# Longformer attention and a gated feed-forward block on one core: scores by two 64-row matmuls in row tiles, and another order of the opening

## The chip, the cores and the metric

The kernel runs on one core of a Trainium2 chip. The metric is the device time of one execution in microseconds (us). The engines are TensorE (matmuls; its weight loads are a row of their own), VectorE, ScalarE, GpSimd and SyncE (which issues DMAs); each takes its instructions in program order. Matmuls write to PSUM, eight banks of 128 partitions x 512 fp32 values; ScalarE and VectorE read them from there.

## The reference

Attention with a window of 32 to each side and 8 global positions, for 8 batches x 8 heads of 576 positions x 64, then a feed-forward block over all 4608 tokens.

```python
def _attn_ref(q, k, v, global_idx):
    scores = scale * np.matmul(q, k.transpose(0, 1, 3, 2))
    mask = np.abs(pos[:, None] - pos[None, :]) <= 32
    mask = mask | is_global[:, None] | is_global[None, :]
    scores = np.where(mask, scores, -1000000000.0)
    attn = softmax(scores)
    return np.matmul(attn, v)

def _moe_ref(x, w_in, w_out):        # x: 4608 x 512
    h = x @ w_in                     # 512 x 2048
    g = h * np.cos(h)
    return g @ w_out                 # 2048 x 512
```

## The kernel before

**Tiles.** Heads are worked on in pairs: 32 pairs, four to a batch, the two heads of a pair in partitions 0 to 63 and 64 to 127. The queries of a pair are cut into 11 blocks of 56, with the 8 global queries ahead of each block (C = 64 columns); the keys of a block are 128 rows: 8 global ones and a window of 120. In `kw` the two heads' keys lie under each other. In `qb` each head has its own half, and the other head's partitions are zero there, so that one matmul over 128 rows gives both heads' scores of a block.

**Scores, values, turn.** `scores(pr, g)` (line 517) takes four blocks at a time: four matmuls into one bank of tag "s", an exponential on ScalarE, a product with the mask on VectorE into `pm`. `values(pr)` (531) multiplies `pm` with the values `vw` in 22 matmuls, each with 64 columns of weights, so that even and odd blocks use different column halves of the array; VectorE then sums, inverts and scales into `xn`. `turn_x(pr)` (552) transposes `xn` into `xT`; at the last pair of a batch GpSimd copies eight columns of global rows.

**Feed-forward.** `xT` is cut into 9 tiles of 512 tokens. `mlp_in(t, f)` is four matmuls of 512 columns into a bank of tag "h" (two of them), `mlp_act` a cosine on ScalarE and a product on VectorE into `g`, which has two buffers. `mlp_out(t, u)` is a quarter of a sum over 16 blocks for 128 tokens, four matmuls of 512 columns into `po`; the first quarter takes the bank of tag "o" (one bank; "s" too in the tail and where `spare` is set), the fourth copies `po` out, on ScalarE for odd and on VectorE for even blocks of tokens. Below, four such matmuls are a **unit**.

**PSUM.** Three banks "s", two "h", one "o", two for `pv`.

**Order.** It is written out by hand, as strings of steps that are issued as they stand. The opening `FRONT` makes pairs 0 to 7: `k`, `q` bring a pair's keys and queries to their places (transposes on TensorE, copies on ScalarE and VectorE), `C` casts values, `w` (`spread`, 361) lays out values by matmuls with 0/1 matrices, `s`, `p`, `x` are scores, values and turn; `L`, `W`, `O`, `K`, `B`, `A`, `c` issue loads (GpSimd's queue, for `A` and `B` SyncE's), `g` copies global rows on GpSimd, `m` and `t` are `mlp_in` and `mlp_act`. Then come passes 3 to 15. Pass 3 (`MID`) has no attention but keys and queries for the next pairs; passes 4 to 15 work on two pairs each, `a` and `z`, with `FOURTH`, `FIFTH`, `SIXTH` and else `ORDER`. There a "1" is a unit of `mlp_in` with its activation, and a "2" a unit of `mlp_out`; `n` squares `xn` on ScalarE for a later check, `G` issues casting DMAs. The steps "1" and "2" do nothing where their conditions fail:

```python
if ins_q and ins_q[0][0] < ready[0] and ins_q[0][0] < outs_q[0][0] + 2:        # "1"
...
if outs_q and need <= ready[1] and (tail[0] or NTT * NF - len(outs_q) < outs_by[0]):   # "2"
```

so a "1" is at most two token tiles ahead of the first "2" that is open. What is left of the 144 + 144 units runs in the tail, "1" and "2" in turn.

Of the kernel before, what the change touches and what calls it, by code (L numbers as in the profile page):

```python
# [9 lines left out]
FP32 = mybir.dt.float32  # L10
FP16 = mybir.dt.float16
I32 = mybir.dt.int32
AF = mybir.ActivationFunctionType
# [6 lines left out]
P = 128  # L20
# [178 lines left out]
def kernel(  # L199
# [138 lines left out]

    def hold(pr):

        nc.gpsimd.tensor_copy(gate, qb[pr % NK][0:1, 0, 0, G : G + 1])

    def vn16(s):
        return xT[:, s, 6 * TT : 9 * TT].rearrange("p (i n) -> p i n", i=NVT)
# [16 lines left out]
    def spread(pr):  # L361

        new, h0 = vn16(pr // 2), 2 * (pr % 2) * D
        for g0 in range(0, NB, 4):
            n = min(4, NB - g0)
            t = ps.tile([P, 4, P], FP32, tag="s", bufs=3)
            for j in range(g0, g0 + n):
                i = j // 2
                parts = ((2, i), (3, i + 1)) if j % 2 else ((0, i), (1, i - 1))
                nc.tensor.matmul(t[:, j - g0], own[:, pr], vg16[:, 0].rearrange("p h d -> p (h d)"), start=True, stop=False)  # L370
                parts = [(a, x) for a, x in parts if x >= 0]
                for a, x in parts:
                    m = min(VT, S - VT * x)
                    nc.tensor.matmul(t[:, j - g0], shift[0:m, a], new[0:m, x, h0 : h0 + 2 * D],  # L374
                                     start=False, stop=(a, x) == parts[-1])
            copy = nc.vector.tensor_copy if g0 == 4 else nc.scalar.copy
            copy(vw[pr % NV][:, g0 : g0 + n, :, 0:D], t[:, 0:n].rearrange("p n (h d) -> p n h d", h=2))

# [4 lines left out]
                view(vg16[(pr % 16) * G : (pr % 16 + 1) * G, pr // 16, h], (0, NB), (1, D)))  # L383


    mask = keep.tile([P, NB, 2, C], FP16)

    def build_mask():

        kid = work.tile([P, NB], FP32, tag="kid", bufs=1)  # L390
        nc.vector.tensor_copy(kid, kid_i)
        gf = work.tile([P, G], FP32, tag="gf", bufs=1)
        nc.vector.tensor_copy(gf, view(gidx_all, (2, G)))
        eq = work.tile([P, NB, G], FP32, tag="eq", bufs=1)
        nc.vector.tensor_tensor(eq, view(kid, (1, NB), (0, G)), view(gf, (0, NB), (1, G)), ALU.is_equal)
        isg = work.tile([P, NB], FP32, tag="isg", bufs=1)
        nc.vector.tensor_reduce(isg, eq, AX.X, ALU.max)
        ge0 = work.tile([P, NB], FP32, tag="ge0", bufs=1)
# [16 lines left out]
        for h in range(2):  # L415
            nc.vector.tensor_tensor(
                mask[:, :, h, G:], view(nk, (1, NB), (0, QB)), view(band[:, G:], (0, NB), (1, QB)), ALU.mult)
            nc.vector.tensor_scalar(
                mask[:, :, h, 0:G], view(val, (1, NB), (0, G)), own[:, 0:1], None, ALU.mult)
# [11 lines left out]
        for h in range(2):  # L431
            nc.vector.tensor_copy(mask[0:G, :, h, G:], view(one, (0, NB), (0, QB)))


    qgT = keep.tile([P, B * NP, G], FP16)
# [44 lines left out]

    def globals_q(pr):
        qp = qb[pr % NK]
        nc.gpsimd.tensor_copy(qp[0:D, 0, :, 0:G], view(qgT[0:D, pr], (0, NB), (1, G)))
        nc.gpsimd.tensor_copy(qp[D:P, 1, :, 0:G], view(qgT[D:P, pr], (0, NB), (1, G)))

    def turned(src, pr, n):

# [14 lines left out]
            nc.vector.tensor_copy(to, view(kT[pr // 2 % 2][:, pr % 2], (QB, NB), (1, W)))  # L502

    def local_q(pr):
        if pr < 2 * HY:
            t = turned(qn[pr // 2 % 2], pr, QP)
        for h in range(2):
            hp = slice(h * D, (h + 1) * D)
            to = qb[pr % NK][hp, h, :, G:]
            if pr < 2 * HY:  # L510
                copy = nc.scalar.copy if h == 0 or pr == 1 else nc.vector.tensor_copy
                copy(view(to, (C, NB), (RW, QB // RW), (1, RW)),  # L512
                     view(t[hp], (QB // RW, NB), (1, QB // RW), (QP, RW)))
            else:
                nc.vector.tensor_copy(to, view(qT[pr // 2 % 2][hp, pr % 2], (QB, NB), (1, QB)))  # L515

    def scores(pr, g):
        kp, qp = kw[pr % NK], qb[pr % NK]
        if g == 0:
            pm_of[pr] = work.tile([P, NB, 2, C], FP16, tag="pm", name="pm")  # L520
        pm = pm_of[pr]
        g0, n = 4 * g, min(4, NB - 4 * g)
        st = ps.tile([P, 4, P], FP32, tag="s", bufs=3)
        for j in range(n):
            nc.tensor.matmul(st[:, j], kp[:, g0 + j], view(qp[:, :, g0 + j], (NB * C, 2), (1, C)), start=True, stop=True)  # L525
        e = work.tile([P, 4, P], FP16, tag="e", bufs=3)
        nc.scalar.activation(e[:, :n], st[:, :n], AF.Exp, scale=scale)  # L527
        nc.vector.tensor_tensor(  # L528
            view(pm[:, g0], (1, n * P)), view(e, (1, n * P)), view(mask[:, g0], (1, n * P)), ALU.mult)

    def values(pr):
        pm, vp = pm_of.pop(pr), vw[pr % NV]
        for j in range(NB):
            for h in range(2):
                r0 = (j % 2) * C
                c0 = ((j // 2) % 3) * 130 + h * 65
                nc.tensor.matmul(pv[r0 : r0 + C, j // 6, c0 : c0 + 65], pm[:, j, h], vp[:, j, h],  # L537
                                 start=True, stop=True)
        den = pv[:, :, D : D + 1]
        rp = r_all[:, pr]  # L540
        dg = work.tile([G, 2], FP32, tag="dg")
# [10 lines left out]
    def turn_x(pr):  # L552
# [2 lines left out]
        if p == 0:  # L555
            xg_of[b] = work.tile([P, NP, G], FP16, tag="xg", name="xg")
        xg = xg_of[b]
        tx = ps.tile([P, BP, P], FP16, tag="o" if front[0] else "s", bufs=1 if front[0] else 3)
        for n in range(BP):
            nc.tensor.transpose(tx[:, n], xn[:, n], ident16)  # L560
        with nc.allow_low_precision("six rows of fp16"):
# [133 lines left out]
    with tc.manual_schedule():  # L695
# [14 lines left out]
        gather(k, kg32, 0)  # L710
        gather(q, qg32, 0)
        gather(v, vg32, 0)
        for t in (kn[1], qn[1], qb[2], qb[3]):
            nc.scalar.memzero(t.rearrange("p a b c -> p (a b c)"))
        load_qk(1)
        for i in range(2):
            nc.vector.memset(qb[i], 0.0)
        build_shifts()
        for i in range(NV):
            nc.vector.memset(vw[i][:, :, :, D : D + 1], 1.0)  # L720
# [53 lines left out]
                 "w": spread, "C": cast_vn, "V": lambda _: hold(9), "A": later_rows, "D": later_globals, "O": load_w_out, "K": lambda s: cast_half(s, "kq" if s == 4 else "vkq"), "B": bring, "m": lambda _: one(False), "t": lambda _: mlp_act()}  # L774
        ready[0] = 1
        for step in FRONT.split():
            f = (STEPS | OTHER)[step[0]]
            f(*[int(x) for x in (step[1:] or "0").split(".")])
        ready[0], front[0] = 2, False
# [85 lines left out]
```

## Time and profile before

| | us |
|---|---|
| median of 3 runs | 370.12 (365.66 to 370.38) |
| profiled run | 371.58 |
| its span | 369.8 |
| TensorE busy | 335.9 (91%) |
| VectorE busy | 266.3 (72%) |
| ScalarE busy | 249.5 (67%) |
| GpSimd busy | 105.9 (29%) |
| pass 3 begins (first steps behind the opening) | 72.4 |
| pass 4 begins | 87.95 |
| tail begins | 290.3 |
| last matmul ends | 363.4 |

The page gives busy time by engine, the span in 40 slices of 9.2 us, a chain of work followed back from the last instruction, and groups of instructions by line. Views of the trace give busy time in chosen stretches, instructions in order of time for one engine, and the same chain in order of time. A line such as `171.88 0.61 PE st L525 x11` reads: from 171.88 us on, for 0.61 us, eleven matmuls of line 525 that write `st`. In groups, `out<-in partitions x elements xcount | busy us, mean ns of one | idle before`.

### The profile page before, as it was taken

The numbers are of one execution on the slowest core, as the hardware profiler recorded it, in microseconds if no ns is written. First come the engines' busy times: TensorE is split into PE (matmuls) and PEld (weight loads), VectorE is DVE, ScalarE is ACT, GpSimd is POOL, SyncE is SP. The second block draws the span as 40 slices with busy tenths as digits, with TensorE's granted clock in tenths as the row PEclk, the third lists the DMA queues.
The fourth block names the chain that finished last, engine by engine and source line by source line (L and its number), as shares of the span: only waits on it lengthen the run. The fifth ranks groups of instructions, "written<-read, shape, count | busy, mean of one in ns | idle before, by whom it ended". The sixth has DMA issues, their size and how long they took to land.

```text
span 369.8 us, 8014 instructions
## 1 busy us (share of the span) xinstructions
PE 335.9 (91%) x2934; PEld 184.9 (50%) x2934; DVE 266.3 (72%) x615; ACT 249.5 (67%) x384; POOL 105.9 (29%) x239
## 2 busy tenths in 40 slices
PE   0399883999998999999999999999999999999992
PEld 0277673545553545555555555555555444444441
DVE  7659974696888888888888888888878445455410
ACT  5488882679776677778777868677787756644300
POOL 6735670161335250705253252603000100000000
PEclk9999997899999999999999999999999999999999
DMA  5979999999999999999999999999920000100111
GB/s 92 197 129 159 180 165 107 198 176 147 102 161 105 194 126 195 125 169 138 195 161 159 160 142 165 160 202 118 130 59 31 28 30 28 57 30 28 53 64 65
DMA packets 176280, 45.57 MB, mean 123 GB/s; under 512 B 164937, under 2 KB 171337, under 8 KB 176041
## 3 DMA queue, kind: packets, MB, share of 16 engines
q1 hardware_dynamic: 112601, 27.61, 58.3%
q0 software_dynamic: 63632, 17.37, 50.3%
q8 instruction: 25, 0.41, 0.5%
q14 instruction: 22, 0.18, 0.2%
HBM read 45.07 MB, written 20.05 MB: 176 GB/s over the span
## 4 chain that ended last, share of the span: by engine, by line
PE 79%; DVE 6%; issue 5%; ACT 3%; POOL 3%; DMA 2%; POOLq 0%; ACTq 0%
PE po L595 32%; PE ph L578 30%; PE st L525 5%; PE pv L537 4%; PE tx L560 2%; PE t L374 2%; DMA qn<-in_q_dram 2%; DVE g L585 2%; ACT e L527 1%; PE t L370 1%; PE t L492 1%; PE pn L628 1%; DVE xn L548 1%; POOL q L262 1%; ACT qb L512 1%
## 5 line engine op out<-in xcount | busy, mean ns | idle before, releaser
L584 ACT ACTIVATE cos<-ph,pio 128x512 f16<-128x512 f32 x144 | 97.1, 687 | 66.3 <-PE ph L578 64.7
L595 PE MATMUL po<-w_out,g 128*128 128x512 f16 x576 | 141.6, 379 | 0.0
L578 PE MATMUL ph<-xT,w_in 128*128 128x512 f16 x576 | 140.1, 379 | 0.3 <-DVE g L585 0.2
L585 DVE TENSOR_TENSOR g<-cos,ph 128x512 f16<-128x512 f16 x144 | 95.9, 685 | 46.9 <-ACT cos L584 44.9
L595 PEld LDWEIGHTS <-g 128*128 128x128 f16 x576 | 55.2, 98 | 62.1
L578 PEld LDWEIGHTS <-w_in 128*128 128x128 f16 x576 | 53.6, 98 | 60.5 <-issue 1.3
L527 ACT ACTIVATE e<-st 128x512 f16<-128x512 f32 (+1 forms) x96 | 47.9, 561 | 15.5 <-PE st L525 9.4
L528 DVE TENSOR_TENSOR pm<-e,mask 128x512 f16<-128x512 f16 (+1 forms) x96 | 37.2, 405 | 22.8 <-ACT e L527 21.0
L752 POOL COPY gate<-xn 1x1 f16<-1x1 f16 x12 | 2.2, 181 | 132.3 <-DVE xn L548 132.3
L525 PE MATMUL st<-qb,kw 128*128 128x128 f16 x352 | 29.2, 223 | 9.4 <-issue 5.0
L525 PEld LDWEIGHTS <-kw 128*128 128x128 f16 x352 | 24.1, 100 | 19.8 <-issue 9.1
L548 DVE TENSOR_TENSOR xn<-pv,r_all 128x768 f16<-128x768 f32 x32 | 30.7, 958 | 1.7
L568 POOL COPY xT<-xg 128x4 f16 x64 | 19.6, 306 | 28.7 <-DVE xT L563 25.3
L262 POOL DMA_DIRECT2D q<-in_q_dram x12 | 26.2, 2181 | 0.0
L614 ACT ACTIVATE sq<-xn 128x1536 f16<-128x1536 f16 x16 | 23.6, 1476 | 0.0
L515 DVE COPY qb<-qT 64x616 f16<-64x616 f16 x48 | 22.1, 460 | 0.3
L374 PE MATMUL t<-xT 112*128 112x128 f16 (+1 forms) x168 | 21.1, 240 | 0.7 <-ACT xT L349 0.4
L600 ACT COPY o<-po 128x512 f32<-128x512 f32 x18 | 10.5, 586 | 15.5 <-PE po L595 15.1
L262 POOL DMA_DIRECT2D k<-in_k_dram x12 | 19.8, 1646 | 0.0
L370 PE MATMUL t<-vg,xT 128*128 128x128 f16 x88 | 18.4, 242 | 0.9 <-issue 0.6
L537 PE MATMUL pv<-vw,pm 128*64 128x65 f16 x704 | 18.5, 199 | 0.0
L602 DVE COPY o<-po 128x512 f32<-128x512 f32 x18 | 12.3, 685 | 6.9 <-PE po L595 6.9
(123 smaller groups left out, 326.8 us busy)
## 6 DMA issues: line engine op xcount, KB each, us to landing
out_dram<-o SPq DMA_DIRECT2D x36, 256.0 KB
vw<-v SPq DMA_DIRECT2D x35, 165.0 KB
v<-in_v_dram POOLq DMA_DIRECT2D x12, 288.0 KB, 4.3
k<-in_k_dram POOLq DMA_DIRECT2D x12, 288.0 KB, 9.2
q<-in_q_dram POOLq DMA_DIRECT2D x12, 288.0 KB, 15.8
vn<-in_v_dram SPq DMA_DIRECT2D x20, 112.0 KB
w_in<-in_moe_w_in_dram POOLq DMA_DIRECT2D x4, 512.0 KB, 12.3
w_out<-in_moe_w_out_dram POOLq DMA_DIRECT2D x1, 2048.0 KB
```

The costliest lines, as they stand in the source:

```text
L262: nc.gpsimd.dma_start(dst[s].rearrange("t (h d) -> t h d", h=4), dview(src, base, (D, S), (S * D, 4), (1, D)))
L374: nc.tensor.matmul(t[:, j - g0], shift[0:m, a], new[0:m, x, h0 : h0 + 2 * D], start=False, stop=(a, x) == parts[-1])
L525: nc.tensor.matmul(st[:, j], kp[:, g0 + j], view(qp[:, :, g0 + j], (NB * C, 2), (1, C)), start=True, stop=True)
L527: nc.scalar.activation(e[:, :n], st[:, :n], AF.Exp, scale=scale)
L528: nc.vector.tensor_tensor(view(pm[:, g0], (1, n * P)), view(e, (1, n * P)), view(mask[:, g0], (1, n * P)), ALU.mult)
L537: nc.tensor.matmul(pv[r0 : r0 + C, j // 6, c0 : c0 + 65], pm[:, j, h], vp[:, j, h], start=True, stop=True)
L548: nc.vector.tensor_tensor(view(xn, (384, 2), (D, 6), (1, D)), view(pv, (512, 2), (65, 6), (1, D)), view(rp, (6, 2), (1, 6), (0, D)), ALU.mult)
L578: nc.tensor.matmul(ph, w_in16[:, j, f * P : (f + 1) * P], xT[:, j, t * TT : (t + 1) * TT], start=(j == 0), stop=(j == NC - 1))
L584: nc.scalar.activation(cos, ph, AF.Sin, bias=pio2)
L585: nc.vector.tensor_tensor(g, cos, ph, ALU.mult)
L595: nc.tensor.matmul(po, g16[:, f, s * P : (s + 1) * P], w_out16[:, f], start=(f == 0), stop=(f == NF - 1))
L614: nc.scalar.activation(sq, view(xn, (1, 2 * BP * P)), AF.Square, accum_out=x_sq[:, s : s + 1])
```

## The change

The zeros in `qb` go: both heads' queries lie under each other as the keys do, and a block's scores are two matmuls over 64 partitions each, one in the upper and one in the lower rows of the array. Each head has banks of its own: two for the blocks 0 to 7 and two for 8 to 10, three of them of tag "s" and one of tag "h" ("o" in the opening). A pair's scores are one step now. The exponentials are two of 512 and two of 192 columns. The values take even and odd blocks in turn, `spread` joins its matmuls, `mask` has one head, and all order strings are new.

```diff
-ORDER = "sa0 sa1 sa2 2 2 2 sz0 2 sz1 sz2 pa 1 1 2 xa pz G 1 1 2 xz n 1 1 2 kc qc 1 kd qd 2 1"
+ORDER = "sa 2 2 2 sz pa 1 1 2 xa pz G 1 1 2 xz n 1 1 2 kc qc 1 kd qd 2 1"
-FOURTH = "2 2 sa0 sa1 sa2 2 sz0 2 sz1 sz2 pa 1 1 2 xa pz G 1 1 2 xz n 1 1 2 kc qc 1 kd qd 2 1"
-FIFTH = "sa0 sa1 sa2 2 2 2 sz0 2 sz1 sz2 pa 1 2 xa pz G 1 2 xz n 1 2 kc qc 1 kd qd 2"
-SIXTH = "sa0 sa1 sa2 2 2 2 sz0 2 sz1 sz2 pa 1 1 2 xa pz G 1 1 2 xz n 1 1 D0 2 kc qc D1 1 kd qd D2 2 1"
-FRONT = ("s0.0 s0.1 s0.2 k1 q1 C0 w0 s1.0 s1.1 s1.2 L2 p0 k2 q2 C1 w1 x0 s2.0 s2.1 s2.2 W0 p1 k3 q3 C2 w2 x1 "
-         "s3.0 s3.1 s3.2 L3 W1 A g4 g5 p2 k4 q4 w3 x2 s4.0 s4.1 s4.2 g6 g7 c4 K4 W2 W3 p3 k5 q5 C3 w4 x3 s5.0 s5.1 s5.2 p4 k6 q6 w5 x4 n0 "
-         "s6.0 s6.1 s6.2 K5 p5 k7 q7 w6 x5 B4 s7.0 s7.1 s7.2 O p6 w7 n1 x6 m p7 m x7 t t")
+FOURTH = "2 2 sa 2 sz pa 1 1 2 xa pz G 1 1 2 xz n 1 1 2 kc qc 1 kd qd 2 1"
+FIFTH = "sa 2 2 2 sz pa 1 2 xa pz G 1 2 xz n 1 2 kc qc 1 kd qd 2"
+SIXTH = "sa 2 2 2 sz pa 1 1 2 xa pz G 1 1 2 xz n 1 1 D0 2 kc qc D1 1 kd qd D2 2 1"
+FRONT = ("s0 k1 q1 C0 w0 s1 L2 k2 q2 C1 w1 p0 s2 W0 k3 q3 x0 C2 w2 p1 s3 L3 W1 A g4 g5 k4 q4 x1 w3 p2 "
+         "s4 g6 g7 c4 K4 W2 W3 k5 q5 x2 C3 w4 p3 s5 k6 q6 x3 w5 p4 s6 K5 k7 q7 x4 w6 p5 s7 B4 O w7 x5 n0 p6 + m m x6 p7 t t m m x7 t t n1 -")
...
-    qb = [keep.tile([P, 2, NB, C], FP16, name=f"qb{i}") for i in range(NK)]
+    qb = [keep.tile([P, NB, C], FP16, name=f"qb{i}") for i in range(NK)]
...
-            for j in range(g0, g0 + n):
-                i = j // 2
-                parts = ((2, i), (3, i + 1)) if j % 2 else ((0, i), (1, i - 1))
-                nc.tensor.matmul(t[:, j - g0], own[:, pr], vg16[:, 0].rearrange("p h d -> p (h d)"), start=True, stop=False)
...
+            nc.tensor.matmul(view(t, (1, n * P)), own[:, pr], view(vg16[:, 0].rearrange("p h d -> p (h d)"), (0, n), (1, P)),
+                             start=True, stop=False, skip_group_check=True)
+            for a, j, k, x in runs:
+                m = min(VT, S - VT * x)
+                nc.tensor.matmul(view(t[:, j], (2 * P, k), (1, P)), shift[0:m, a], new[0:m, x : x + k, h0 : h0 + 2 * D],
+                                 start=False, stop=(a, j, k, x) == runs[-1], skip_group_check=True)
...
-        nc.gpsimd.tensor_copy(qp[0:D, 0, :, 0:G], view(qgT[0:D, pr], (0, NB), (1, G)))
-        nc.gpsimd.tensor_copy(qp[D:P, 1, :, 0:G], view(qgT[D:P, pr], (0, NB), (1, G)))
+        nc.gpsimd.tensor_copy(qp[:, :, 0:G], view(qgT[:, pr], (0, NB), (1, G)))
...
     def local_q(pr):
+        to = qb[pr % NK][:, :, G:]
         if pr < 2 * HY:
             t = turned(qn[pr // 2 % 2], pr, QP)
+            copy = nc.scalar.copy if pr % 2 else nc.vector.tensor_copy
+            copy(view(to, (C, NB), (RW, QB // RW), (1, RW)),
+                 view(t, (QB // RW, NB), (1, QB // RW), (QP, RW)))
+        else:
+            nc.vector.tensor_copy(to, view(qT[pr // 2 % 2][:, pr % 2], (QB, NB), (1, QB)))
+
+    def scores(pr):
+        kp, qp = kw[pr % NK], qb[pr % NK]
+        pm = pm_of[pr] = work.tile([P, 2, NB, C], FP16, tag="pm", name="pm")
+        tags = (("s", 3), ("s", 3), ("s", 3), ("o", 1) if front[0] else ("h", 2))
+        st = [ps.tile([P, 512], FP32, tag=tag, bufs=bufs, name="st") for tag, bufs in tags]
+        for j in range(NB):
+            for h in range(2):
+                hp = slice(h * D, (h + 1) * D)
+                nc.tensor.matmul(st[j // 8 * 2 + h][:, j % 8 * C : j % 8 * C + C], kp[hp, j], qp[hp, j], start=True, stop=True)
         for h in range(2):
-            hp = slice(h * D, (h + 1) * D)
...
+            e = work.tile([P, 512], FP16, tag="e", bufs=3)
+            nc.scalar.activation(e, st[h], AF.Exp, scale=scale)
+            nc.vector.tensor_tensor(view(pm[:, h], (1, 512)), e, view(mask, (1, 512)), ALU.mult)
+        e = work.tile([P, 512], FP16, tag="e", bufs=3)
+        n = (NB - 8) * C
+        for h in range(2):
+            nc.scalar.activation(e[:, h * n : (h + 1) * n], st[2 + h][:, 0:n], AF.Exp, scale=scale)
+        nc.vector.tensor_tensor(view(pm[:, 0, 8], (NB * C, 2), (1, n)), view(e, (n, 2), (1, n)), view(mask[:, 8], (0, 2), (1, n)), ALU.mult)
...
-        for j in range(NB):
+        for j0 in range(0, NB, 2):
             for h in range(2):
...
-        tx = ps.tile([P, BP, P], FP16, tag="o" if front[0] else "s", bufs=1 if front[0] else 3)
+        tx = ps.tile([P, BP, P], FP16, tag="s", bufs=3)
...
-        for t in (kn[1], qn[1], qb[2], qb[3]):
+        for t in (kn[1], qn[1]):
...
-        for i in range(2):
-            nc.vector.memset(qb[i], 0.0)
```

`spare`, set between "+" and "-", lets two of four `mlp_in` steps take a bank of tag "s". `MID` and the limits `outs_by` (8 more "2" with each pass) are as before.

More of the change, by code (lines that the diff above doesn't have):

```diff
@@ L339, in hold @@
     def hold(pr):
-        nc.gpsimd.tensor_copy(gate, qb[pr % NK][0:1, 0, 0, G : G + 1])
+        nc.gpsimd.tensor_copy(gate, qb[pr % NK][0:1, 0, G : G + 1])
     def vn16(s):
@@ L383, in load_vg @@
                 view(vg16[(pr % 16) * G : (pr % 16 + 1) * G, pr // 16, h], (0, NB), (1, D)))
-    mask = keep.tile([P, NB, 2, C], FP16)
+    mask = keep.tile([P, NB, C], FP16)
     def build_mask():
@@ L414, in build_mask @@
         nc.vector.memset(own[0:G], 0.0)
[L415 to L419, printed above, removed]
+        nc.vector.tensor_tensor(
+            mask[:, :, G:], view(nk, (1, NB), (0, QB)), view(band[:, G:], (0, NB), (1, QB)), ALU.mult)
+        nc.vector.tensor_scalar(
+            mask[:, :, 0:G], view(val, (1, NB), (0, G)), own[:, 0:1], None, ALU.mult)
         gc = work.tile([G, 1], FP32, tag="gc", bufs=1)
@@ L430, in build_mask @@
         nc.vector.tensor_scalar(one, one, 0.5, None, ALU.is_le)
-        for h in range(2):
-            nc.vector.tensor_copy(mask[0:G, :, h, G:], view(one, (0, NB), (0, QB)))
+        nc.vector.tensor_copy(mask[0:G, :, G:], view(one, (0, NB), (0, QB)))
     qgT = keep.tile([P, B * NP, G], FP16)
@@ L504, in local_q @@
     def local_q(pr):
+        to = qb[pr % NK][:, :, G:]
         if pr < 2 * HY:
             t = turned(qn[pr // 2 % 2], pr, QP)
-        for h in range(2):
-            hp = slice(h * D, (h + 1) * D)
[L509 to L529, printed above, removed]
+            copy = nc.scalar.copy if pr % 2 else nc.vector.tensor_copy
@@ L531, in values @@
     def values(pr):
         pm, vp = pm_of.pop(pr), vw[pr % NV]
-        for j in range(NB):
+        for j0 in range(0, NB, 2):
             for h in range(2):
[L535 to L538, printed above, removed]
+                for j in range(j0, min(j0 + 2, NB)):
+                    r0 = (j % 2) * C
+                    c0 = ((j // 2) % 3) * 130 + h * 65
+                    nc.tensor.matmul(pv[r0 : r0 + C, j // 6, c0 : c0 + 65], pm[:, h, j], vp[:, j, h],
+                                     start=True, stop=True)
@@ L776 @@
         for step in FRONT.split():
+            if step in "+-":
+                spare[0] = step == "+"
+                continue
+            if step in "+-":
+                spare[0] = step == "+"
+                continue
             f = (STEPS | OTHER)[step[0]]
```

10 lines of the change are left out of this document (5 added, 5 removed).

## The prediction

> **What bounds the kernel now.** I read the engine slices and the chain of waits first, then busy time by stage, then one middle pass on TensorE, ScalarE and VectorE. The page:
>
> ```profile
> PE   0399883999998999999999999999999999999992
> ...
> PE 79%; DVE 6%; issue 5%; ACT 3%; POOL 3%; DMA 2%; POOLq 0%; ACTq 0%
> ```
>
> TensorE carries the chain; its only hole after the first slices is the 3 in slice seven. By stage (opening until 72.40, then pass 3, passes 4 to 15, the tail):
>
> ```profile
> 16.70:57.25 40.55, 35.60 (x696) 29.91 (x696) 31.26 (x76) 33.54 (x56) 23.02 (x44) 1.00 1.23 158
> 57.25:62.29 5.04, 0.00 (x0) 0.00 (x0) 0.75 (x3) 0.00 (x0) 0.00 (x0) 0.85 1.72 86
> 62.29:72.40 10.11, 9.44 (x108) 6.89 (x108) 5.86 (x17) 6.42 (x10) 0.00 (x0) 0.74 1.68 185
> 72.40:87.95 15.55, 15.32 (x71) 6.74 (x69) 13.87 (x26) 12.57 (x20) 8.62 (x24) 1.00 1.66 167
> 87.95:290.30 202.35, 200.48 (x1691) 107.12 (x1690) 170.71 (x388) 153.55 (x229) 63.24 (x149) 1.00 1.38 140
> 105.48:121.21 15.73, 13.97 (x127) 7.27 (x126) 13.35 (x30) 11.95 (x18) 5.59 (x12) 1.00 1.41 146
> 155.58:172.50 16.92, 16.92 (x143) 9.06 (x142) 14.49 (x34) 12.92 (x20) 6.82 (x16) 1.00 1.60 153
> 290.30:363.40 73.10, 72.93 (x339) 32.65 (x336) 31.23 (x57) 35.00 (x57) 0.00 (x0) 1.00 0.12 44
> ```
>
> Columns: length, then busy time of TensorE, its weight loads, VectorE, ScalarE and GpSimd, granted clock, DMA share, GB/s. From 72.40 on TensorE is never free. Pass 5 (105.48) is the exception that matters: it has 12 units where the others have 16, and still takes 15.73. A unit is one step "1" or "2", four matmuls of 512 columns. So when units are taken out of a pass, another chain soon holds it. One pass on TensorE, as the chain of waits has it:
>
> ```profile
> 155.58 2.59 PE po L595 x12
> ...
> 159.64 0.50 PE pv L537 x22
> 160.14 1.83 PE ph L578 x8
> 161.97 0.86 PE po L595 x4
> 162.84 0.34 PE tx L560 x6
> ...
> 166.70 1.73 PE ph L578 x8
> ...
> 171.88 0.61 PE st L525 x11
> ```
>
> A unit is 0.865 us (1.73 for two). 16 units are 13.84; the other 3.08 of 16.92 are two scores (0.61 each), two values (0.50), two turns (0.34) and twice 0.10: two units behind the values, which use half the array's columns, take 1.83 instead of 1.73. That 0.10 is the price of leaving a tiled mode.
>
> **Scores in row tiles.** 22 matmuls of 64 columns in place of 11 of 128. No row shows 64-row tiles. The nearest is the values: 22 matmuls of 65 columns in column tiles take 0.50; less 0.10 for the way in, 0.40, or 18 ns each. I take 0.40 and 0.10 for each change of mode: 0.60 for pair a of a pass, 0.50 for z (its way out is the way into the values). That is 1.10 against 1.22, 0.12 less a pass. The far bound is no overlap at the old pace: 0.61/11 = 55 ns, 22 of them 1.22, about 0.7 more a pair. [...]
>
> **Fewer "2" in a pass.** The order loses a "2" with the merged score steps: seven a pass, not eight. Walking the strings with the conditions of `one` and `two` gives, for passes 4 to 15, 92 "1" and 96 "2" before, 82 and 84 after; ten "1" are refused, since a "1" may be at most two token tiles ahead of the "2" (two in pass 5, two in 8, four in 10, two in 12). Pass 3 keeps its 18 and the opening gets 4 instead of 2. So 22 units leave the passes, 20 go to the tail. The tail has 80 units and four of the norms in 73.10, 0.870 each: **+17.4 us**. The passes must give that back, and TensorE alone would: 22 x 0.865 = 19.0.
>
> **What holds the passes then.** ScalarE and VectorE in that pass:
>
> ```profile
> 155.00 0.69 ACT L584 ACTIVATE cos<-ph,pio 128x512 f16<-128x512 f32 x1 [0.28 <-PE ph L578]
> 155.71 1.28 ACT L527 ACT_TABLE_LOAD   x1
> 157.00 2.02 ACT L527 ACTIVATE e<-st 128x512 f16<-128x512 f32 x4
> 159.51 0.98 ACT L527 ACTIVATE e<-st 128x512 f16<-128x512 f32 x2 [0.49 <-DVE pm L528]
> 160.51 1.28 ACT L584 ACT_TABLE_LOAD   x1
> ```
>
> ```profile
> 155.33 0.93 DVE L515 COPY qb<-qT 64x616 f16<-64x616 f16 x2
> ...
> 157.63 1.23 DVE L528 TENSOR_TENSOR pm<-e,mask 128x512 f16<-128x512 f16 x3 [0.65 <-ACT e L527]
> ...
> 160.80 0.15 DVE L542 TENSOR_REDUCE dg<-pv 8x2 f32<-8x12 f32 x1
> ...
> 161.44 0.96 DVE L548 TENSOR_TENSOR xn<-pv,r_all 128x768 f16<-128x768 f32 x1
> ```
>
> ```profile
> L527 ACT ACTIVATE e<-st 128x512 f16<-128x512 f32 x64 | 36.0, 596 | 15.5 <-PE st L525 9.4 <-DVE pm L528 5.9
> L527 ACT ACTIVATE e<-st 128x384 f16<-128x384 f32 x32 | 15.8, 492 | 0.0
> L600 ACT COPY o<-po 128x512 f32<-128x512 f32 x18 | 10.5, 586 | 15.5 <-PE po L595 15.1
> L602 DVE COPY o<-po 128x512 f32<-128x512 f32 x18 | 12.3, 685 | 6.9 <-PE po L595 6.9
> ```
>
> Let T be the start of a pass's scores (here 155.58 - 0.61 = 154.97). The first exponential starts at T+2.0, behind the last cosine and the table load. Four of them take 2.02 with one at 0.596, so one follows another by 0.48. 128 columns cost 0.104 (596 - 492 ns), so 192 columns follow by 0.22, and a pair's exponentials are 2 x 0.48 + 2 x 0.22 = 1.4 (before 0.48 + 0.48 + 0.37 = 1.3). After: pair a until T+3.4; z from T+3.6, when its scores are there (0.60 + three units + most of 0.50), until T+5.0; the products run 0.4 each behind them (1.23 for three), the last until T+5.5; from dg 0.64 until xn, which takes 0.96: T+7.1. There TensorE has come by T+6.8 (0.60, 0.50 and 0.50 of scores and values, six units) and waits 0.3; turn 0.34, values 0.50: T+8.0; then nine units and a turn, 8.1. A pass with all "1" is **16.1**, where its TensorE work is 16.92 - 0.865 - 0.12 = 15.9. One 0.46 copy of the queries less on VectorE for each pair is worth nothing here: it sits under the wait for ScalarE.
>
> **A wait that seven "2" make.** `po` has one bank ("o") in the passes. Before, each fourth part falls between sz0 and sz1 or at a pass's end, with values or scores before the next part 0. With seven a pass it drifts. In passes 5, 9 and 13 it is the first "2" after sa, in 6, 10 and 14 the second; the next "2" is a part 0 and waits for the copy of `po`. That copy stands behind pair a's four exponentials on ScalarE (odd quarters) or its three products on VectorE (even ones), and behind TensorE's wait stand sz, the values, everything. The exponentials are through at T+3.5, the products at T+4.0, so copies end at T+3.5+0.59 = T+4.1 (ScalarE) or T+4.0+0.69 = T+4.7 (VectorE); TensorE is there at T+1.4 (first) or T+2.3 (second). Passes 5: 2.7; 9: 3.3; 10: 2.4; 14: 1.8. In 6 and 13 no cosine comes just before, the exponentials start at T+0.45, and 0.8 and 1.1 remain. Sum **12.1**. In 7, 11 and 15 the copy is third and pushes z's work by 0.4: 1.2; two smaller ones (12, 14): 0.9. The ten refused "1" give back less than their 8.6: in pass 8 they lie ahead of xn's T+7.1 and give nothing, in 5, 10 and 12 about 3.1, 1.9 and 1.8. Passes 4 to 15: 12 x 16.1 + 12.1 + 1.2 + 0.9 - 6.8 = 200.6, **-1.7** against 202.35. [...]
>
> **The opening.** Chain of waits:
>
> ```profile
> 13.68 0.68 ACT qb L512
> ...
> 14.38 0.81 DVE qb L512
> ...
> 16.40 0.27 POOL qb L484
> ...
> 19.96 0.66 ACT qb L512
> ...
> 20.64 0.67 ACT qb L512
> ...
> 57.25 5.04 issue
> 62.29 1.01 PE st L525 x8
> ```
>
> The first scores lose ScalarE's 0.68 ahead of the global rows and one GpSimd copy, 0.27 and its gap: 1.3. Pair 1 loses one of two copies, 0.67. In pairs 2 to 7 VectorE's 0.81 goes from every second one: 3 x 0.8 at most where VectorE sets the pace, of which I count 2.0. The dropped memsets of `qb` and the half of the mask run while the first loads are awaited: nothing. `spread` moves the same columns in 16 instead of 32 matmuls. The later x steps take their turns, VectorE copies and GpSimd column copies along, past scores and values, and K5 and the w_out load behind x3's copies on GpSimd's queue; I keep that at nothing, since w_out is needed first in pass 4. At 57.25 TensorE stops for 5.04 inside a row of scores, waiting for nothing the profile shows, and the clock granted behind it is 0.74. If the stop ends when it did, only what now lies ahead of it is saved, at least the 1.01 of scores: -1.0; if it goes, 1.3 + 0.67 + 2.0 + 5.04: -9.0. I take **-4.0**, the gain with the stop moved along, the two more units in the opening paid where TensorE waits now.
>
> **Sum**: -1.7 + 17.4 - 4.0 = +11.7. The profiled run took 371.58 (span 369.8): 383.3; on the median 370.12 it is **382**.
>
> **Rivals.**
> - TensorE stays the bound in all passes, because the copies of `po` come sooner than by the queue order above. Passes 166 x 0.865 + 12 x (3.08 - 0.12) = 179.1, -23.2; with +17.4 and -4.0 it is -9.8: 360. For it: TensorE has no hole in the pass shown. Against: pass 5 before, 12 units in 15.73. It decides if the six waits come to less than about 2 us together. Chance 0.13.
> - A middle: the stop in the opening goes (-9) and half of the 12.1 is hidden: +0.7, 371. Chance 0.17.
> - Row tiles do not overlap: 1.22 for a pair, plus 0.1 to 0.2, 0.6 more than forecast for 32 pairs: +19, 401; half-way, 28 ns each (0.61/22), 388. For it: nothing here shows two row tiles. Against: the values. Chance 0.13.
> - The forecast, 374 to 392: 0.57.
>
> **How the numbers follow.** 2% of 370 is 7.4 us, about what a measurement of this kernel tells from no change. Slower: 0.57 less 0.04 for its lower edge, plus 0.13: 0.66. Within: 0.17 + 0.04 = 0.21. Faster: 0.13. Range 364 to 396: it leaves out 0.10 of the fast case and about 0.07 of the slowest.
>
> **What would show it.** In the profile after: `po` waiting for ScalarE's or VectorE's copy for some 10 us in six passes of 12, long holes behind the scores; the tail near 90 us (104 units); scores near 0.5 to 0.6 a pair; exponentials of 192 columns near 0.34. Wrong would be passes of 15.9 throughout, scores over 0.9, or an opening that ends (first `po`) outside 79 to 86 us.

## The result, and the profile after

The changed kernel takes 394.81 us (median of 4 runs, 393.04 to 398.08), the kernel before, measured beside it, 368.15: a ratio of 1.074 (95% interval 1.061 to 1.086), some 27 us slower. Ratios here and below leave out executions that took over 1.5% longer than the fastest of the same kernel. The profiled run took 396.42 (span 394.6), 24.8 more than the one before.

The page of the changed kernel: TensorE and granted clock by slices, the chain of waits by engine, and the group of the `po` matmuls (the last column is TensorE's idle time ahead of them):

```profile
PE   0399889999769999769788998989999999999993
...
PEclk9999999999898999988989999999999999999998
...
PE 61%; ACT 14%; DVE 12%; issue 4%; DMA 4%; SPq 2%; POOL 2%; ACTq 0%; DVEq 0%; POOLq 0%
...
L596 PE MATMUL po<-w_out,g 128*128 128x512 f16 x576 | 146.7, 389 | 13.7 <-DVE o L603 7.4
```

The hole of the opening is gone, and there are holes from slice eleven to slice 27 instead, and the clock's row has 8s between slices 11 and 21. TensorE's share of the chain falls from 79% to 61%; ScalarE and VectorE have what it lost.

By stage, the first unit of `po` (start of pass 4 but for its scores) and then stretches from one pass's scores to the next:

```profile
81.80 1.89 PE L596 MATMUL po<-w_out,g 128*128 128x512 f16 x8
```

```profile
98.94:118.18 19.24, 12.72 (x138) 5.88 (x138) 12.89 (x27) 10.92 (x17) 4.69 (x7) 0.91 1.25 135
118.18:137.10 18.92, 18.08 (x162) 8.31 (x163) 13.10 (x31) 12.14 (x24) 7.76 (x18) 0.91 1.50 142
137.10:153.84 16.74, 16.47 (x161) 8.22 (x161) 13.27 (x31) 12.85 (x21) 5.19 (x10) 1.00 1.58 137
153.84:170.88 17.04, 14.30 (x155) 7.26 (x154) 12.56 (x30) 11.71 (x19) 6.52 (x15) 1.00 1.64 164
170.88:193.20 22.32, 18.58 (x161) 8.94 (x162) 13.55 (x32) 12.86 (x21) 5.86 (x12) 0.85 1.44 145
193.20:211.87 18.67, 14.21 (x146) 7.09 (x145) 13.19 (x27) 11.18 (x19) 5.81 (x13) 0.91 1.23 129
211.87:228.40 16.53, 16.35 (x160) 8.05 (x161) 14.43 (x33) 12.20 (x20) 5.34 (x11) 1.00 1.61 126
...
297.60:388.42 90.82, 90.20 (x418) 40.54 (x416) 37.45 (x67) 41.68 (x66) 0.00 (x0) 1.00 0.12 45
```

These are passes 5 to 11 and the tail. The reader is to see two kinds of pass: 7 and 11 take 16.5 to 16.7, while 5, 6, 9 and 10 take 18.7 to 22.3 at a granted clock of 0.85 to 0.91. The tail is 17.7 longer than the 73.10 before.

What the `po` matmuls wait for, in us, times and longest, by the view of waits:

```profile
PE po L596 <- DVE o L603: 7.4, 5, 3.2
...
PE po L596 <- ACT o L601: 6.2, 4, 2.7
```

And two of these waits on TensorE in order of time, at the heads of passes 5 and 9, with the head of pass 6 between them:

```profile
98.94 0.49 PE L520 MATMUL st<-qb,kw 64*128 64x64 f16 x22
99.36 1.04 PE L596 MATMUL po<-w_out,g 128*128 128x512 f16 x4
103.10 3.27 PE L596 MATMUL po<-w_out,g 128*128 128x512 f16 x8 [2.70 <-ACT o L601]
106.31 0.49 PE L520 MATMUL st<-qb,kw 64*128 64x64 f16 x22
...
118.18 0.50 PE L520 MATMUL st<-qb,kw 64*128 64x64 f16 x22 [2.03 <-DVE qb L510]
118.61 2.67 PE L596 MATMUL po<-w_out,g 128*128 128x512 f16 x8
...
175.56 3.57 PE L596 MATMUL po<-w_out,g 128*128 128x512 f16 x8 [3.22 <-DVE o L603]
```

One unit goes behind pair a's scores, and then nothing for 2.70 or 3.22 us. On VectorE one sees what the second wait is for: the copy of `po` (L603) stands third, behind all of pair a's products.

```profile
173.61 0.91 DVE L524 TENSOR_TENSOR pm<-e,mask 128x512 f16<-128x512 f16 x2 [1.22 <-ACT e L523]
174.54 0.36 DVE L529 TENSOR_TENSOR pm<-e,mask 128x384 f16<-128x384 f16 x1
174.82 0.68 DVE L603 COPY o<-po 128x512 f32<-128x512 f32 x1
```

Two things beside the wait can be read from TensorE's rows. Eight matmuls behind a stop take 3.27, 2.67 or 3.57 us where the same eight take 1.89 at 81.80: they run at half pace for all or part of the time (the granted clock is 0.50 from 102.53 to 105.94, from 119.60 to 123.01 and from 174.21 to 181.04). And pass 6's scores start 2.03 late, behind the queries' copy. That copy is queued behind a copy of the keys which takes 3.03 us, six times the 0.52 of the next; VectorE, and GpSimd's row for the same time:

```profile
114.62 3.03 DVE L500 COPY kw<-kT 128x1320 f16<-128x1320 f16 x1
117.58 0.45 DVE L510 COPY qb<-qT 128x616 f16<-128x616 f16 x1
117.95 0.52 DVE L500 COPY kw<-kT 128x1320 f16<-128x1320 f16 x1
```

```profile
114.04 1.64 POOL L261 DMA_DIRECT2D k<-in_k_dram  x1
115.11 2.19 POOL L261 DMA_DIRECT2D q<-in_q_dram  x1
```

GpSimd issues two casting loads from 114.04 to 117.30, and the slow copy lies beside them. The same happens at 208.05 (3.30 us), ahead of pass 11. Before, the longest of these copies took 1.62.

### The profile page after: what moved, and what is told of

Same layout as the page of the kernel before. It is cut to its first block, busy times and chain, and to the rows that moved or that the text cites. A ratio compares the mean times of both kernels' runs of the same rounds, so it can differ in the third digit from the quotient of the medians.

```text
span 394.6 us, 8415 instructions
## 1 busy us (share of the span) xinstructions
PE 345.0 (87%) x3158; PEld 173.1 (44%) x3158; DVE 254.6 (65%) x583; ACT 246.0 (62%) x409; POOL 95.1 (24%) x207
## 4 chain that ended last, share of the span: by engine, by line
PE 61%; ACT 14%; DVE 12%; issue 4%; DMA 4%; SPq 2%; POOL 2%; ACTq 0%; DVEq 0%; POOLq 0%
PE po L596 25%; PE ph L579 22%; ACT e L523 4%; DVE g L586 3%; PE t L375 3%; PE pv L538 3%; ACT cos L585 3%; PE st L520 3%; PE tx L561 2%; DVE xn L549 2%; DVE kw L500 2%; ACT e L528 2%; DMA kn<-in_k_dram 2%; DMA vg<-in_v_dram,gidx_rows 1%; ACT L523 1%
## 5 line engine op out<-in xcount | busy, mean ns | idle before, releaser
L596 PE MATMUL po<-w_out,g 128*128 128x512 f16 x576 | 146.7, 389 | 13.7 <-DVE o L603 7.4
L579 PE MATMUL ph<-xT,w_in 128*128 128x512 f16 x576 | 141.8, 380 | 2.6 <-DVE g L586 0.9
L596 PEld LDWEIGHTS <-g 128*128 128x128 f16 x576 | 56.2, 99 | 82.8 <-issue 20.9
L524 DVE TENSOR_TENSOR pm<-e,mask 128x512 f16<-128x512 f16 x64 | 26.6, 424 | 42.8 <-ACT e L523 41.2
L523 ACT ACTIVATE e<-st 128x512 f16<-128x512 f32 x64 | 34.8, 598 | 26.2 <-PE st L520 25.8
L561 PE MATMUL tx<-ident,xn 128*128 128x128 f16 x192 | 16.5, 223 | 7.0 <-DVE xn L549 6.9
L601 ACT COPY o<-po 128x512 f32<-128x512 f32 x18 | 10.7, 595 | 18.9 <-PE po L596 18.8
L520 PE MATMUL st<-qb,kw 64*128 64x64 f16 x704 | 18.3, 198 | 4.4 <-DVE qb L510 2.0
L520 PEld LDWEIGHTS <-kw 64*128 64x128 f16 x704 | 14.0, 99 | 16.7 <-issue 9.1
L561 PEld LDWEIGHTS <-xn 128*128 128x128 f16 x192 | 11.8, 99 | 17.6 <-DVE xn L549 15.5
L375 PE MATMUL t<-xT 112*128 112x256 f16 (+2 forms) x104 | 18.4, 287 | 1.3 <-DVE xT L347 1.2
L500 DVE COPY kw<-kT 128x1320 f16<-128x1320 f16 x24 | 18.8, 781 | 0.0
```

Source lines behind the costliest of these rows:

```text
L375: nc.tensor.matmul(view(t[:, j], (2 * P, k), (1, P)), shift[0:m, a], new[0:m, x : x + k, h0 : h0 + 2 * D], start=False, stop=(a, j, k, x) ...
L520: nc.tensor.matmul(st[j // 8 * 2 + h][:, j % 8 * C : j % 8 * C + C], kp[hp, j], qp[hp, j], start=True, stop=True)
L523: nc.scalar.activation(e, st[h], AF.Exp, scale=scale)
L579: nc.tensor.matmul(ph, w_in16[:, j, f * P : (f + 1) * P], xT[:, j, t * TT : (t + 1) * TT], start=(j == 0), stop=(j == NC - 1))
L596: nc.tensor.matmul(po, g16[:, f, s * P : (s + 1) * P], w_out16[:, f], start=(f == 0), stop=(f == NF - 1))
```

## The experiments

Three questions: is it the "2" that the passes lost, and if so, the units that go to the tail or the place of a fourth quarter in a pass? What do the lowered clock and the slow key copies cost? And what did the row tiles and the new opening do by themselves?

### Eight "2" a pass again (e1_eight)

```diff
-ORDER = "sa 2 2 2 sz pa 1 1 2 ...
+ORDER = "sa 2 2 2 sz 2 pa 1 1 2 ...
```

`FOURTH`, `FIFTH` and `SIXTH` likewise.

> The changed kernel with the eighth "2" put back in every pass, between sz and pa, where the kernel before has one; nothing else differs. If the drift of the quarters of po is what costs (my account), the fourth quarter falls between sz and pa again, no matmul waits for a copy of po, 80 units are left for the tail (73 us) instead of 100, a full pass is TensorE's own 16 x 0.865 + about 2.75 = 16.6, and the time is 362 (359 to 366), below both kernels. If the row tiles and the bank of tag h that scores take hold the passes by themselves, full passes stay at 17.5 or more and the time at 372 or more. If moving units to the tail is what costs, the tail is shorter by 17 and the passes grow by nearly as much: 385 or more.

362.63 us, ratio to before 0.983 (0.971 to 0.995): 32 us less than the changed kernel by one "2" a pass, and faster than the kernel before. A pass in the middle, by busy time and on TensorE:

```profile
182.49:199.40 16.91, 16.91 (x167) 8.35 (x166) 13.56 (x32) 12.98 (x21) 6.48 (x15) 1.00 1.58 158
...
284.00:357.00 73.00, 72.90 (x338) 32.67 (x336) 31.20 (x57) 34.95 (x56) 0.00 (x0) 1.00 0.12 44
```

```profile
182.49 0.49 PE L520 MATMUL st<-qb,kw 64*128 64x64 f16 x22
182.92 2.76 PE L596 MATMUL po<-w_out,g 128*128 128x512 f16 x12
185.62 0.60 PE L520 MATMUL st<-qb,kw 64*128 64x64 f16 x22
186.15 1.04 PE L596 MATMUL po<-w_out,g 128*128 128x512 f16 x4
```

TensorE is busy for the whole pass, three units run through behind pair a's scores, and the tail is at 73.0 again. One pass, the seventh, is long (20.9): its values wait 1.4 us for a load of `vw`, and the matmuls behind run at half pace (eight take 3.54 at 135.25, and 1.90 at 140.47).

### Seven "2" in the kernel before (e2_before_seven)

```diff
-ORDER = "sa0 sa1 sa2 2 2 2 sz0 2 sz1 sz2 pa ...
+ORDER = "sa0 sa1 sa2 2 2 2 sz0 sz1 sz2 pa ...
```

> The kernel before with the "2" between sz0 and sz1 taken out of every pass: seven a pass, all else as before. My account: the same drift, the same six passes with TensorE waiting for a copy of po (10 to 15 us), the granted clock under 1 in them, a tail of 90 us; 390 to 400. If the row tiles or the new opening are what makes the changed kernel slow, this one stays within 6 us of the kernel before, 362 to 375.

394.93 us, ratio 1.073 (1.057 to 1.088); `po` waits 7.1 us for VectorE and 5.7 for ScalarE. Without row tiles, new banks or the new opening, the missing "2" alone makes a loss of the same size. The equal total hides one difference: here the first `po` comes at 86.03, 4.2 later than in the changed kernel, and from pass 4's scores to pass 15's it is 192.9 against 197.1; one reason is that only one of its stops is followed by matmuls at half pace (eight take 3.46 at 177.29, and 1.89 behind the stop that ends at 107.02).

### Same number of "2", other places (e7_shifted, e9_copy_ahead)

`e7_shifted` has eight in every pass, but one less in pass 4, so that a fourth quarter stands behind pair a's scores in each of passes 5 to 15. `e9_copy_ahead` keeps the changed kernel's seven and moves two of them ahead of the scores.

```diff
-FOURTH = "2 2 sa 2 sz pa 1 1 2 xa pz G 1 1 2 xz n 1 1 2 kc qc 1 kd qd 2 1"
+FOURTH = "2 2 sa 2 sz 2 pa 1 1 2 xa pz G 1 1 2 xz n 1 1 2 kc qc 1 kd qd 1"
```

```diff
-ORDER = "sa 2 2 2 sz pa ...
+ORDER = "2 2 sa 2 sz pa ...
```

> e1_eight with one "2" less in pass 4 alone: seven there, eight in every pass from 5 on, so that each of these passes begins with a fourth quarter behind pair a's scores (always an odd block, copied by ScalarE) and a first quarter behind it. First theory, it is the place of the fourth quarter in the pass that costs: po waits about 2.7 us for ScalarE in ten passes and about 0.8 in pass 6, 28 us together, and the time is 388 to 399, though only one unit has moved to the tail. Rival, what costs is the number of units left for the tail: 362 to 365 and no such waits.

> The changed kernel, still seven "2" a pass, with two of the three "2" that stand behind sa put ahead of it in every pass ("2 2 sa 2 sz" throughout, as pass 4 has it), so that the copy of po stands ahead of pair a's exponentials on its engine. First theory, the copy's place in the queue behind the exponentials made the waits: po waits 2 to 4 us in all instead of 13.6, the lowered clock goes with them but for the stop behind the slow key copies, and the time is 378 to 384. It stays above the kernel before, since the tail keeps its 104 units. Rival, seven a pass is what costs, wherever they stand: 391 to 396.

`e7_shifted` takes 400.25 us, ratio 1.092 (1.083 to 1.100), just above the upper end of what was expected; one unit more in the tail and 38 us more than `e1_eight`. Its view of waits, and TensorE at the heads of passes 8 to 12:

```profile
PE po L596 <- ACT o L601: 28.6, 12, 2.7
```

```profile
154.59 1.89 PE L596 MATMUL po<-w_out,g 128*128 128x512 f16 x8 [2.70 <-ACT o L601]
...
174.33 3.46 PE L596 MATMUL po<-w_out,g 128*128 128x512 f16 x8 [2.70 <-ACT o L601]
...
195.65 1.89 PE L596 MATMUL po<-w_out,g 128*128 128x512 f16 x8 [2.71 <-ACT o L601]
...
215.40 3.41 PE L596 MATMUL po<-w_out,g 128*128 128x512 f16 x8 [2.70 <-ACT o L601]
...
236.66 1.89 PE L596 MATMUL po<-w_out,g 128*128 128x512 f16 x8 [2.70 <-ACT o L601]
```

28.6 us of waits where 28 were expected: the place decides, not the count. Most of the other 9 us is half pace behind five of the stops (3.4 to 3.5 us for eight matmuls instead of 1.89, 7.7 together). `e9_copy_ahead` is the other half of the proof: 382.72, ratio 1.037 (1.029 to 1.045), 12 us under the changed kernel with the same number of units everywhere. Its `po` waits are 5.5 (3.9 for VectorE, 1.6 for ScalarE; 2 to 4 were expected). That it stays 13 us above the kernel before is the other loss: 20 units more in the tail than `e1_eight` has left (100 instead of 80, 17.4 us at 0.87), less what the shorter passes give back. The 104 in the expectations counts the four units of the norms, which every tail has, and their 24 follows from it.

### The lowered clock and the slow copies (e3_fill, e4_hold, e8_fill_hold, e10_ahead_hold)

`e3_fill` puts spare matmuls, into columns of `pv` that nothing reads, behind the fourth quarters where TensorE waits. `e4_hold` lets GpSimd issue the casting loads of passes 5 and 10 only when the last queries of the pass are copied. `e8_fill_hold` does both, `e10_ahead_hold` the second on `e9_copy_ahead`.

```diff
+                elif step == "f":
+                    for _ in range(FILL[s][1]):
+                        nc.tensor.matmul(pv[:, 0, 390:512], ident16, w_in16[:, 0, 0:122], start=True, stop=True)
```

```diff
+            if s in (5, 10):
+                steps[steps.index("G")] = "Y"                # global rows only
+                steps.insert(steps.index("qd") + 1, "Z")     # hold(2 * s + 3), then the loads
```

> The changed kernel with 12 to 55 spare matmuls of 122 columns (into unused columns of pv, about 54 ns each, never longer than the wait) behind the fourth quarter of po in passes 5, 6, 9, 10, 13 and 14. The copy of po comes as late as before; only TensorE is not idle before it. If the lowered clock behind the waits is a cost of its own, the granted clock stays at 1.00 through passes 9 and 10 but for what other stops leave, and the time falls by 3 to 6: 389 to 392 against 395. If the wait alone counts, 394 to 396.

> The changed kernel with GpSimd's casting loads of passes 5 and 10 (step G without its global rows) issued only after the queries of pair d are copied, by a one-element copy that waits for them. If the two kw copies of 3 us on VectorE are long because GpSimd issues those loads at the same time, no kw copy is over 1.7 us, the scores of passes 6 and 11 start some 2.5 us earlier each and run at full clock: 389 to 391. If they are long for another reason, they stay at 3 us and the time at 394 to 396.

> The changed kernel, seven "2" a pass, with both the spare matmuls behind the fourth quarters of e3_fill and the held casting loads of e4_hold. First theory, the lowered clock behind the waits (4.8 us) and the slow key copies (3.8 us) are two separate losses: 385 to 387.5. Rival, they are one and the same (the clock falls because of the stop behind the slow copies): 389 to 391.

> e9_copy_ahead with the casting loads of passes 5 and 10 held as in e4_hold. First theory, the slow key copies cost another 3 to 5 us there too: 374 to 380, and what is left against e1_eight, 12 to 17 us, is the tail's 24 units less what the shorter passes give back. Rival, without the waits the copies have slack: within 1 us of e9_copy_ahead.

| | us | ratio to before (95%) |
|---|---|---|
| changed kernel | 394.81 | 1.074 (1.061 to 1.086) |
| e3_fill | 390.00 | 1.060 (1.049 to 1.070) |
| e4_hold | 390.97 | 1.064 (1.053 to 1.075) |
| e8_fill_hold | 387.62 | 1.055 (1.044 to 1.067) |
| e9_copy_ahead | 382.72 | 1.037 (1.029 to 1.045) |
| e10_ahead_hold | 385.11 | 1.045 (1.032 to 1.057) |

With the waits filled, 4.8 us go although the copies of `po` come as late as before: that is the half pace behind the waits. The four runs have a mean granted clock of 0.992 to 0.993, those of the changed kernel 0.972 to 0.981. With the loads held, the key copies take 0.53 again, as the row of `e4_hold` below shows in place of the 3.03 above, and 3.8 us go. In its profile pass 5 takes 17.05 instead of 19.24 and pass 10 16.83 instead of 18.67, but pass 10 has lost its half pace there too (1.02 behind its wait instead of 1.68).

```profile
113.59 0.52 DVE L500 COPY kw<-kT 128x1320 f16<-128x1320 f16 x1
```

Both together give 7.2 of the 8.6 that the two give alone: nearer to two losses than to one, though 387.62 lies between what the two theories gave, and the intervals overlap. The profiles decide it. Passes 5 and 10 run at a granted clock of 1.00 both in `e3_fill` (first two lines) and in `e8_fill_hold` (last two), and the held loads still make them 2.10 and 0.97 shorter, 3.1 together:

```profile
96.18:114.03 17.85, 13.73 (x183) 8.03 (x182) 12.87 (x27) 10.92 (x17) 4.68 (x7) 1.00 1.28 142
187.32:205.12 17.80, 15.19 (x185) 8.50 (x185) 13.19 (x27) 11.17 (x19) 5.79 (x13) 1.00 1.57 130
...
98.19:113.94 15.75, 13.66 (x182) 8.01 (x181) 10.78 (x28) 10.92 (x17) 1.12 (x4) 1.00 1.33 131
187.17:204.00 16.83, 15.13 (x185) 8.47 (x184) 11.19 (x28) 10.32 (x17) 1.01 (x5) 1.00 1.32 138
```

On `e9_copy_ahead` the hold gives nothing: its first theory falls. The key copies are short there too (0.56 on average, against 0.79), but in that order two units stand between them and the next scores, and the stop at pass 6's scores was only 0.31 us.

### Row tiles and the opening (e6_rows128, e5_old_front)

Both start from `e1_eight`.

```diff
-nc.tensor.matmul(st[...], kp[hp, j], qp[hp, j], start=True, stop=True)
+nc.tensor.matmul(st[...], kp[:, j], qp[:, j], start=True, stop=True)
```

> e1_eight with the scores over all 128 rows, the same 22 matmuls into the same banks, so there is no row tile and each score mixes both heads' products (another result of the scores, the same work behind them). First theory, two row tiles overlap and the change of mode eats most of it: 22 matmuls take 0.58 to 0.62 us a pair instead of 0.31 and two changes of about 0.1 each, the pass stays at 16.9 to 17.1 and the time within 361 to 366. [...] Second rival, they save half of the scores' time for nothing: 0.3 a pair, 24 pairs in the passes, 370 or more.

> The changed kernel with eight "2" a pass as in e1_eight, but with the opening's steps in the order that they had before (scores still one step, in row tiles; two "1" in the opening instead of four, so pass 5 takes four instead of two). First theory, the order of the steps took the 6 us out of the opening: the first po comes at 85 to 88 us again and the time is 366 to 369. Rival, the dropped copies and memsets of the queries and the shorter scores took them: the first po stays at 79 to 82 and the time at 361 to 364.

Over all rows the time is 363.44, ratio 0.990 (0.981 to 0.998): not to be told from `e1_eight`. The profile can tell:

```profile
128.19 0.80 PE L520 MATMUL st<-qb,kw 128*128 128x64 f16 x22
128.83 2.75 PE L596 MATMUL po<-w_out,g 128*128 128x512 f16 x12
```

From the first score to the first matmul behind it are 0.64 us, against 0.43 in `e1_eight` (182.49 to 182.92) for pair a, and 0.71 against 0.53 for pair z. The way out of the row tiles takes a part of that back. In the chain of waits the three units behind pair a take 2.70 in `e1_eight` and 2.59 over all rows:

```profile
182.99 2.70 PE po L596 x12
...
163.66 2.59 PE po L596 x12
```

The pass is 17.09 against 16.90. So the two row tiles do overlap, and 0.1 a pair is left of it. Whether it is the matmuls or their weight loads that overlap is not separated: for all scores the matmuls are busy for 18.4 us against 28.0, the weight loads for 13.9 against 26.1.

With the old order of the opening the ratio is 0.994 (0.988 to 1.000), some 4 us above `e1_eight`, though the two intervals overlap; in its profile, of an execution of 369.06 us, the stop and the late start of the passes are back:

```profile
61.34 0.38 PE L539 MATMUL pv<-vw,pm 128*64 128x65 f16 x6 [4.46 <-issue]
...
85.84 1.89 PE L597 MATMUL po<-w_out,g 128*128 128x512 f16 x8
```

The three profiles with an old order of the opening (before, `e2_before_seven`, this one) have a stop of 4.5 to 5.0 us on TensorE in which it waits for nothing that the profile shows; none of the eleven with the new order has one over 2.2. So it is the order that took the stop away. What the stop is stays open.

### A better version (e11_eight_tuned, e12_eight_hold)

`e12_eight_hold` is `e1_eight` with the loads of pass 5 held as above. `e11_eight_tuned` also issues each pair's global rows of `vw` ahead of its window rows.

> e1_eight with two more edits against its one long pass (20.9 us instead of 16.9): the casting loads of pass 5 held until pair 13's queries are there, and each pair's global rows of vw loaded ahead of its window rows. First theory, the 1.9 us wait for the load of vw and the lowered clock behind it go: 358 to 360.5. Rival, the loads land as late as before or the held casts make the next transposes late: 361.5 to 365.

> e1_eight with the casting loads of pass 5 alone held until pair 13's queries are there; the loads of vw stay in their order. First theory, of the two edits of e11_eight_tuned it was the new order of vw's loads that made the later passes longer (17.4 to 17.9 us instead of 16.9), and the hold alone gives passes of 16.9 and 360 to 362.5. Rival, the held casts come too late for the passes behind: long passes from pass 7 on and 364 to 368.

`e11_eight_tuned` takes 366.13 (ratio 0.994, 0.989 to 0.998): a miss. Pass 7 is down to 17.4, but five waits for the window rows of `vw` came instead, and passes 9, 10, 11 and 13 take 17.4 to 17.9. `e12_eight_hold` takes 363.34, a little over what was expected, ratio 0.985 (0.980 to 0.990), so it is faster than the kernel before by 1.5%, and has the shortest span of the profiles, 359.6:

```profile
81.74:263.31 181.57, 180.14 (x1776) 88.98 (x1776) 144.91 (x333) 138.36 (x229) 55.17 (x119) 1.00 1.45 153
```

From pass 4's scores to pass 15's TensorE is free for 1.4 us. Whether it beats `e1_eight` can't be told: 0.985 against 0.983.

## Why the prediction was right, and where it was too small

The direction and the mechanism held; the sum, +11.7, was less than half of the +24.8 between the two profiled spans. The measured 394.81 lies above the forecast's own bounds, 374 to 392, and only 1.2 us inside the range to 396. The upper end of the range was made for scores that do not overlap, which the runs refute, so that it held was in part luck. By its terms:

**The tail.** Forecast +17.4, measured +17.7 (90.82 against 73.10). `e1_eight`, with 80 units left, has 73.00.

**The opening.** Forecast -4.0, measured -6.0 (87.78 to 81.80). The stop went, which the forecast had only as its far end. But with the stop gone the forecast would have had -9.0; two units more in the opening (1.7 us) and the moved x steps, which I had counted at nothing, lie in between. `e5_old_front`, with two units fewer in its opening, gives the order of the steps about 4 us of it, and about 2 are left for the dropped copies (87.78 to 85.84); each is read from one profile.

**The waits for `po`.** Sized one by one, and this is the part that held best: passes 5, 6, 9, 10, 13, 14 were to wait 2.7, 0.8, 3.3, 2.4, 1.1 and 1.8, 12.1 together; they wait 2.70, 0.67, 3.22, 2.35, 1.02 and 1.84, 11.8. The other 1.9 of the 13.6 are three short waits in passes 5, 8 and 14 (0.74, 0.76 and 0.37). `e7_shifted` and `e9_copy_ahead` show that it is the queue order that makes them.

**Row tiles.** Forecast 0.60 and 0.50 for a pair with its changes of mode, 1.10 together; measured in `e1_eight` 0.43 and 0.53, and 0.11 more on the units behind each, 1.2 together. The pass did not get shorter by the 0.12 that was counted: 16.90 in `e1_eight` against 16.92 before, with the same 16 units.

**Passes 4 to 15.** This is the step that failed: "Passes 4 to 15: 12 x 16.1 + 12.1 + 1.2 + 0.9 - 6.8 = 200.6, -1.7". Measured are 215.6 (81.97 to 297.60), +13.3 against 202.35. Spread over the passes by the prediction's own terms (16.1 each, plus the waits, 0.4 in 7, 11 and 15, 0.45 in 12 and 14, less what the refused "1" give):

| pass | 4 | 5 | 6 | 7 | 8 | 9 | 10 | 11 | 12 | 13 | 14 | 15 |
|---|---|---|---|---|---|---|---|---|---|---|---|---|
| forecast | 16.1 | 15.7 | 16.9 | 16.5 | 16.1 | 19.4 | 16.6 | 16.5 | 14.75 | 17.2 | 18.35 | 16.5 |
| measured | 17.0 | 19.2 | 18.9 | 16.7 | 17.0 | 22.3 | 18.7 | 16.5 | 16.0 | 17.5 | 18.8 | 16.9 |

10.5 of the 15 us that are missing lie in passes 5, 6, 9 and 10. Two terms were not in the sum:

- Half pace behind a stop. From the rows: 3.27, 2.67 and 3.57 for eight matmuls instead of 1.89, and two units of four behind other waits (1.53 at 121.95 and 1.68 at 197.88 instead of 1.04): 5.0 us in passes 5, 6, 9 and 10. These four passes are 5.6 shorter together in `e3_fill`, and its time is 4.8 lower. The prediction saw a clock of 0.74 behind the opening's stop, and did not carry it over to the stops that it forecast itself.
- The slow key copies ahead of passes 6 and 11: 3.1 from the lengths of passes 5 and 10 in `e3_fill` and `e8_fill_hold`, 3.8 from the time of `e4_hold`. The rows of before had it as well, with 1.62 for the longest such copy instead of 0.53, under a TensorE that still had work. That the two fall together when a pass shifts against GpSimd's queue was not tested by itself.

The other 6 us are spread. Pass 8 is one place where it shows: the two refused "1" were to give nothing and cost nothing, but its turn waits 1.98 us for `xn` and the pass takes 0.9 more. I did not take these apart further.

**What the removed units give back.** The forecast said that 19.0 would be due and another chain would hold the passes. That is the core of the loss: the plain passes of the changed kernel, 7, 11 and 15, take 16.5 to 16.9 with 15 units, those of `e1_eight` 16.9 with 16. A unit taken out of a pass gave back 0 to 0.4 us, and cost 0.87 in the tail. So `e9_copy_ahead`, with most of the waits gone, still loses 13 us.

**The rivals.** TensorE is not the bound in all passes (360), the row tiles do overlap (401, 388), and though the stop in the opening went as the middle case (371) had it, none of the waits was hidden.

## What to carry to other kernels

When an order written by hand has a cycle of its own (here four quarters to a bank of `po`), count it modulo the pass: with eight steps a pass every fourth quarter stays at its place, a good one in `e1_eight` and a bad one in `e7_shifted`, and with seven it walks through all places, the bad ones among them. Work that is taken out of a stage bound on one engine only pays if nothing else holds the stage at nearly the same length; otherwise it is paid for once more where it goes. And a stop that is forecast has a price beyond its length: here 5.0 us of half pace in four passes, and 3.1 to 3.8 us for key copies that came to lie beside GpSimd's loads.

## What the runs showed of the hardware that was not expected

**Of nine equal stops four were followed by half pace and five were not, and the four come some 41 us apart.** In `e7_shifted` nine stops of 2.70 us stand at the same place of passes 7 to 15. Behind four of them (ending at 174.33, 215.40, 256.40 and 297.38) eight matmuls take 3.4 to 3.5 us, behind the other five 1.89. The four are 41.07, 41.00 and 40.98 apart, two passes of some 19.75 and 21.3. Busy time by stretches shows the clock itself: it falls to 0.50 at 174.13, for 3.41 us, and in the same way at 215.09, 256.05 and 297.01, each 40.96, or 12 times 3.41, behind the one before. In the changed kernel the clock is at 0.50 for 3.41 us from 102.53, from 119.60 and from 198.10, and for 6.83 from 174.21, and these starts are 5, 16 and 7 times 3.41 apart in order of time. So the stops can be laid on a grid of 3.41 us:

```profile
150.24:153.65 3.41, 1.64 (x28) 0.78 (x27) 1.90 (x5) 3.10 (x5) 1.52 (x7) 1.00 2.09 197
153.65:157.06 3.41, 2.48 (x32) 1.17 (x31) 0.78 (x2) 1.10 (x4) 0.00 (x0) 1.00 1.74 163
170.72:174.13 3.41, 0.91 (x4) 0.29 (x3) 1.88 (x5) 3.38 (x7) 0.00 (x0) 1.00 1.73 93
174.13:177.54 3.41, 3.21 (x8) 1.02 (x7) 0.06 (x1) 0.15 (x1) 0.00 (x0) 0.50 2.01 156
```

The stop that ends at 154.59 is shared by two stretches; TensorE is free for 1.77 us in the first, and the clock stays. The stop that ends at 174.33 lies almost whole in one, with 2.50 us free, and the next runs at half. On the grid of each run, from pass 4 to the tail, the fourteen profiles have fifteen such falls, all behind stretches with 1.68 to 2.87 us free; the most that was not followed by a fall is 1.84.

In the changed kernel the stretches ahead of its four falls have 2.13, 2.00, 1.87 and 2.35 us free; the one from 262.96 has 1.84, and the clock stays. A stop of 2.25 us, in pass 5 of `e7_shifted`, was followed by half pace too (3.49 for eight matmuls at 99.17). What makes the clock fall is not shown beyond these numbers.

**A copy of the keys took 0.53 us, and 2.8 to 3.3 beside the issue of two casting loads on GpSimd.** The long ones are 3.03 and 3.30 in the changed kernel and 2.76 in `e1_eight`. With the issue moved away by `e4_hold` and `e12_eight_hold`, none of 24 takes over 0.81. How the issue makes the copy longer is not shown. One of GpSimd's copies is long there too: 1.51 us for the global keys at 209.88 in the changed kernel, where the next of them takes 0.26.

**Row tiles.** 22 matmuls over 64 rows x 64 columns, alternating between the two halves of the array, take 0.43 us up to the next matmul, 0.64 over all 128 rows; the way out costs 0.11 more on the units behind.
